# Middle-stage weights converted seven batches earlier by way of DRAM, and the middle channel product in seven block products

## The chip, the cores and the metric

The kernel runs on one core of a Trainium2 chip. The metric is the device time of one execution, in microseconds (us); the median of three runs of the kernel before is 1297.31 us (1297.03 to 1298.79).

The engines are called by their full names in the text; the profile calls them PE (TensorE matmul), PEld (TensorE weight load), DVE (VectorE), ACT (ScalarE), POOL (GpSimd) and SP (SyncE, which issues the DMAs here).

## The reference, cut to what matters

Three blocks follow each other, on 8 batches of 576 tokens with 512 channels: attention with pooled keys, a mixing block with a token and a channel product, and a second one.

```python
# block 1: x = attention(q, k, v)                    (8, 576, 512)
theta = x @ w_theta                                   # block 2
y = w_tok_r @ (x * cos(theta)) + w_tok_i @ (x * sin(theta))
u = x + y
x = u + maximum(u @ w_ch, 0)                          # 512 x 512: the middle channel product
h = (maximum(x.T @ w_tok1, 0) @ w_tok2).T             # block 3: 576 -> 256 -> 576 over the tokens
u = x + h
out = u + maximum(u @ w_ch1, 0) @ w_ch2               # 512 -> 1536 -> 512 over the channels
```

The weights arrive as float64. There is no such type on the engines, so the kernel takes each number apart in two 32-bit words and puts a float32 together from them with integer operations ("conversion" below).

## The kernel before, in words

**Precision.** A float32 product is made of three faster ones: each operand is split into a high part (a cast on ScalarE) and a low part (the difference, on VectorE or GpSimd), and high x high, high x low and low x high are added up in PSUM. So every matrix needs a cast and a subtraction before it can be used, and every product costs three matmuls. The list `HL3` names the three.

**Stages.** (1) A prologue. (2) The mixing of the eight batches, one after the other: `mix_steps(b)` is the token product of batch b (four row blocks, each in 256 and 320 columns), and `interleave` slips the "side" work in between: attention and theta of batch b+1, loads for b+2. A side step stands beside a due time, in us of a modelled TensorE clock; the constants are in the table `P`. (3) The middle stage: per batch the channel product `ch` with `w_ch`, transposes `emit_tr`, and the two token products `emit_tok1` and `emit_tok2`. (4) The last stage, `channel_mix`, with `w_ch1` and `w_ch2`. The engines run in order; a scheduler behind the language settles the order on each engine when the kernel is built.

**The weights of the middle stage** (`w_ch`, `w_tok1`, `w_tok2`) are converted in 19 pieces while the last batch is mixed: `begin` in the last batch's side work queues them (`add_wch`, `add_tok1`, `add_tok2`), and `cq_step` (L239) does one at a time: four or so VectorE operations (L248 to L271), the cast on ScalarE (L294), the low part on GpSimd or VectorE (L296). They stay in SBUF.

**The middle channel product** (`emit_ch`, L889) multiplies, for each of four output blocks and each of two token ranges (256 and 320), 12 matmuls: four row blocks of `w_ch` times the three high/low pairs. That is 8 groups of 12, or in blocks of half the channels and half the tokens eight block products. One VectorE operation per group takes the result from PSUM: maximum with 0, plus u (L900). `split_u` (L881) makes the high and low parts of the input, four casts and four subtractions of 576 columns a batch.

**The weights of the last stage** are converted beside it: `weight_steps(0, ...)` in six quads of six steps; `wstep()` places a step at six points of a batch. Its sums for seven block products are `sums(i)` (L1033): two on GpSimd (L1037, L1038), two on VectorE (L1039, L1040). `channel_mix` already works with seven block products (`first_pair`, L1262).

Of the kernel before, what the change touches and what calls it, by code (L numbers as in the profile page):

```python
# [56 lines left out]
    "mo": 1,  # L57
}
# [6 lines left out]
def tile_attn_moe(  # L65
# [713 lines left out]

    def mix_steps(b):  # L780
# [11 lines left out]
    def mix_part(b, half, jj, th, part, hold):  # L792
# [16 lines left out]
        if part == 8:  # L809
            R = r_t[b]  # L810
            nc.vector.tensor_add(out=R[:, j, ts], in0=o, in1=R[:, j, ts])  # L811
            if th == 1:
                nc.sync.dma_start(out=scr_u[b][:, j, :], in_=R[:, j, 0:T])
# [16 lines left out]
    wch = [None] * 4  # L830
    A2 = {}

    def add_wch():
        for k in range(4):
            cq_add(pair_tile(("q0", "q1", "pt0", "pt1")[k], 512, f"wch{k}", wch, k),
                   w_ch[k * 128:(k + 1) * 128, :], HALVES)

    def add_tok1():
        def make():
            t = st("e", [128, 2, 5, 256], F32R, "wk1")  # L840
            A2["tok1"] = t
            return t

        get = lazy(make)
        for s in range(4):
            cq_add(lambda s=s: (get()[:, 0, s, :], get()[:, 1, s, :]),
                   w_tok1[s * 128:(s + 1) * 128, :], ((0, 256),))

        def tail(m):
            t = get()  # L850
            nc.scalar.copy(out=t[:, 0, 4, :], in_=m)
            nc.gpsimd.memset(t[64:128, 1, 4, :].bitcast(F32), 0.0)
            nc.gpsimd.tensor_sub(out=t[0:64, 1, 4, :], in0=m[0:64], in1=t[0:64, 0, 4, :].bitcast(F32))

        cq_src.append((w_tok1[512:576, :], 64, tail))

    def add_tok2():
        def make(s):
            if s == 0:
                t = st("kr", [128, 2, T], F32R, "wk2a")  # L860
                t = (t[:, 0], t[:, 1])
            else:
                t = (st("t1", [128, T], F32R, "wk2b"), st("pl", [128, T], F32R, "wk2c"))
            A2["tok2", s] = t
            return t

        for s in range(2):
            cq_add(lazy(lambda s=s: make(s)), w_tok2[s * 128:(s + 1) * 128, :], ((0, 192), (192, 384), (384, 576)))

    u_t = {}  # L870
    uh_t = {}
# [3 lines left out]
    def load_u(b):  # L875
        t = st(("R0", "R1", "Z1")[b % 3], [128, 4, TD], F32, f"u{b}")
        u_t[b] = t
        for j in range(4):
            nc.sync.dma_start(out=t[:, j, 0:T], in_=scr_u[b][:, j, :])

    def split_u(b, j):  # L881
        if j == 0:
            uh_t[b] = (st("Xh", [128, 4, T], F32R), st("Xl", [128, 4, T], F32R))
        h, l = uh_t[b]
        u = u_t[b][:, j, 0:T]
        nc.scalar.copy(out=h[:, j], in_=u)
        nc.vector.tensor_sub(out=l[:, j], in0=u, in1=h[:, j].bitcast(F32))

    def emit_ch(b, j, th):  # L889
        t0, n = TH[th]  # L890
        ts = slice(t0, t0 + n)
        h = uh_t[b]
        o = bank_any()[:, 0:n]
        i = 0
        for a, w in HL3:
            for k in range(4):
                mm(o, wch[k][:, w, j * 128:(j + 1) * 128], h[a][:, k, ts], i == 0, i == 11)
                i += 1
        u = u_t[b][:, j, ts]
        nc.vector.scalar_tensor_tensor(out=u, in0=o, scalar=0.0, in1=u, op0=ALU.max, op1=ALU.add)  # L900
        gate[0] = u[0:1, 0:1]
        if j == 3 and th == 1:
            dup_tail(u_t[b], nc.scalar.copy)
# [56 lines left out]
    A12, A22, S1, S2, S3, S4, A11 = range(7)  # L960
    PO = (A11, S2, A12, S1, S3, S4, A22)
# [15 lines left out]
    def weight_steps(m, wd, tags, gaps):  # L977
# [55 lines left out]
        def sums(i):  # L1033
# [3 lines left out]
            nc.gpsimd.tensor_tensor(out=s[:, 0], in0=a21, in1=a22, op=ALU.add)  # L1037
            nc.gpsimd.tensor_tensor(out=s[:, 2], in0=a11, in1=a21, op=ALU.subtract)  # L1038
# [47 lines left out]
    HOME_E = (("Z1", 5), ("Xh", 3), ("Xl", 3), ("R0", 3))  # L1086
# [454 lines left out]
    if True:  # L1541
        prologue()
        for b in range(B):
# [12 lines left out]
            if last:  # L1556
                def begin():
                    zt = st(f"zt{(b + 1) % 2}", [128, CV, 2], U32, "late0")
                    vs = [st(x, [128, 256, 2], U32, f"late_{x}") for x in ("vbh", "vbl", "vlh", "vll")]
                    vr = st("vr", [128, 3, CV], F32, "late1")  # L1560
                    n = [int(x + 0.5) for x in P["l_n"]]
                    cq_use((["stg0", "stg1", "bdk"] + ([zt] + vs)[0:n[0]]),
                           (["cvt0", "vlr"] + [vr[:, i] for i in range(3)])[0:1 + n[1]])
                    lo_m[0] = max(2, n[2])
                    cq_mode[0] = min(2, int(P["md"][0] + 0.5))
                    add_wch()
                    add_tok1()
                    add_tok2()
                    cq_load()
                side.append((0.0, begin))  # L1570
                for i in range(19):
                    side.append((P["l_cq"][0] + P["l_cq"][1] * i, cq_step))
# [21 lines left out]
        if B > 1:  # L1594
            load_u(1)
# [88 lines left out]
```

## Time and profile before

| what | value |
|---|---|
| median of 3 runs | 1297.31 us |
| the profiled execution's own time | 1297.42 us |
| its span | 1295.6 us |
| TensorE busy | 97% of the span |
| VectorE, ScalarE, GpSimd busy | 74%, 51%, 25% |
| granted TensorE clock, mean | 0.995 |

The span is the time from the first to the last instruction; what lies around it is 1.8 us. TensorE's share is an average over stages with different limits, so stretches are read apart: the mixing runs to about 526 us, the middle stage from there to about 752 us, the last stage from there on.

### The profile page before, as it was taken

Reading aid. Unit: us, or ns where it says so; the run is one execution under the profiler, and the core shown is the slowest. Engines: PE = TensorE matmul, PEld = TensorE weight load, DVE = VectorE, ACT = ScalarE, POOL = GpSimd, SP = SyncE. Lnnn points to the kernel's source line nnn. Section 1 sums busy time; section 2 is a strip of 40 time slices with the busy share of each in tenths; the row PEclk is TensorE's granted clock in tenths of the full one; section 3 lists DMA queues with packets and bytes.
Section 4 is the critical chain, followed back from the end, with each engine's and each line's share of the span. In section 5 each row is a group of like instructions: output and inputs, shape, how many; then the busy total and the mean of one; then the engine's idle time right before and its main releaser. Section 6 shows DMA issues by size and latency. Waiting matters only on the chain.

```text
span 1295.6 us, 22271 instructions
## 1 busy us (share of the span) xinstructions
PE 1254.6 (97%) x8130; PEld 1209.8 (93%) x8132; DVE 956.9 (74%) x1730; ACT 661.0 (51%) x1256; POOL 321.9 (25%) x339
## 2 busy tenths in 40 slices
PE   5799999999999999999999999999999999999998
PEld 4489999999999988899999998999999999999998
DVE  7888577585857796686775689996545598987893
ACT  4776565666666573333331356655544444444442
POOL 4643425232332532111110012320000032123122
PEclk9899999999999999999999999999999999999999
DMA  9424233231321023556683388885438966547621
GB/s 338 158 71 138 74 100 103 75 94 62 115 73 52 36 93 109 181 199 233 246 297 116 128 273 281 281 280 178 146 123 279 367 215 224 172 142 218 196 91 62
DMA packets 120382, 214.50 MB, mean 166 GB/s; under 512 B 11536, under 2 KB 66320, under 8 KB 120272
## 3 DMA queue, kind: packets, MB, share of 16 engines
q1 hardware_dynamic: 120272, 213.08, 49.2%
q8 instruction: 64, 1.05, 0.3%
q14 instruction: 46, 0.38, 0.1%
HBM read 134.39 MB, written 78.64 MB: 164 GB/s over the span
## 4 chain that ended last, share of the span: by engine, by line
PE 76%; DVE 9%; DMA 2%; issue 2%; ACT 2%; POOL 0%; SPq 0%; ACTq 0%; DVEq 0%; POOLq 0%
PE m L159 28%; PE x L159 25%; PE t L159 19%; PE x L173 3%; DMA ws<-w_ch 1%; DMA scr_x<-u 1%; DVE wm L1024 1%; DVE raw_n L1155 1%; DVE wm L1028 1%; DVE wsum L1039 0%; DVE p L1313 0%; DVE g L1323 0%; ACT wo L1052 0%; DVE ope_R L1152 0%; ACT wm L1018 0%
## 5 line engine op out<-in xcount | busy, mean ns | idle before, releaser
L159 PE MATMUL m<-wtk,Z 128*128 128x256 f32 (+1 forms) x1536 | 253.6, 301 | 4.6 <-ACT Z L772 3.0
L159 PEld LDWEIGHTS m<-wtk,Z 128*128 128x128 f32 x1536 | 220.2, 190 | 6.1 <-ACT Z L772 3.2
L773 POOL TENSOR_TENSOR Z<-tmp,Z 128x1024 fp32r<-128x1024 f32 x31 | 74.9, 2415 | 112.1 <-ACT Z L772 112.1
L159 PE MATMUL x<-ope_Z,wa 128*128 128x384 f32 x492 | 95.4, 337 | 0.0
L1404 POOL TENSOR_TENSOR o<-o,u 128x384 f32<-128x384 f32 x12 | 16.3, 1379 | 285.5 <-DVE u L1392 218.0
L159 PEld LDWEIGHTS x<-ope_Z,wa 128*128 128x128 f32 x492 | 86.8, 188 | 0.1
L1038 POOL TENSOR_TENSOR wsum<-wm 128x128 f32<-128x128 f32 (+1 forms) x18 | 15.1, 840 | 272.4 <-DVE wm L1028 264.8
L758 DVE TENSOR_TENSOR tmp<-x,tmp 128x1024 f32<-128x1024 f32 x32 | 39.1, 1221 | 33.4 <-ACT tmp L734 17.8
L159 PE MATMUL t<-wth,Xh 128*128 128x256 f32 x448 | 62.9, 282 | 0.0
L159 PE MATMUL x<-bdk,q 128*128 128x144 f32 x320 | 47.8, 303 | 11.5 <-DVE bdk L1463 7.0
L159 PEld LDWEIGHTS t<-wth,Xh 128*128 128x128 f32 x448 | 57.9, 188 | 0.9 <-DVE tmp L709 0.2
L159 PEld LDWEIGHTS x<-bdk,q 128*128 128x128 f32 x320 | 44.5, 203 | 13.1 <-issue 10.9
L159 PE MATMUL m<-wtk,zt 128*128 128x256 f32 (+1 forms) x192 | 56.8, 296 | 0.0
L557 POOL TENSOR_TENSOR e<-e,sm 128x720 f32<-128x720 f32 x32 | 44.7, 1398 | 20.8 <-DVE sm L556 18.7
L159 PE MATMUL t<-ope_Z,wa 128*128 128x384 f32 x234 | 48.2, 336 | 1.5 <-ACT p L1312 1.5
L159 PE MATMUL m<-ope_Z,wa 128*128 128x384 f32 x234 | 48.2, 336 | 0.0
L740 DVE SCALAR_TENSOR_TENSOR tmp<-tmp,t 128x512 f32<-128x512 f32 x33 | 22.5, 683 | 31.3 <-ACT tmp L727 31.3
L545 ACT ACTIVATE e<-e 128x720 f32<-128x720 f32 x32 | 25.6, 804 | 38.0 <-DVE e L540 37.9
L159 PE MATMUL x<-ope_R,wa 128*128 128x384 f32 x228 | 44.1, 338 | 0.4 <-DVE p L1317 0.3
L811 DVE TENSOR_TENSOR R<-m,R 128x256 f32<-128x256 f32 (+1 forms) x64 | 28.8, 450 | 20.2 <-PE m L159 20.2
L772 ACT CAST Z<-tmp 128x1024 fp32r<-128x1024 f32 x32 | 33.4, 1043 | 20.0 <-DVE tmp L758 20.0
L159 PE MATMUL m<-ope_Xl,wa 128*128 128x384 f32 x204 | 42.9, 338 | 0.6 <-ACT ope_Xl L1151 0.6
(406 smaller groups left out, 3546.3 us busy)
## 6 DMA issues: line engine op xcount, KB each, us to landing
wa<-scr_w SPq DMA_DIRECT2D x42, 512.0 KB, 5.6
scr_g<-g SPq DMA_DIRECT2D x108, 192.0 KB, 3.0
scr_w<-wo SPq DMA_DIRECT2D x42, 256.0 KB, 3.0
scr_u<-R SPq DMA_DIRECT2D x32, 288.0 KB, 2.1
u<-scr_u SPq DMA_DIRECT2D x32, 288.0 KB, 4.0
scr_w<-wo SPq DMA_DIRECT2D x18, 512.0 KB, 3.4
scr_x<-u SPq DMA_DIRECT2D x32, 288.0 KB, 2.4
raw_n<-scr_x SPq DMA_DIRECT2D x24, 384.0 KB, 4.3
```

The lines of the kernel that those rows point to most:

```text
L159: nc.tensor.matmul(out=o, lhsT=l, rhs=r, start=start, stop=stop, skip_group_check=skip)
L173: nc.tensor.transpose(o, i, ident)
L545: nc.scalar.activation(out=ep, in_=ep, func=ACTF.Exp, scale=1.0 / 64.0)
L557: nc.gpsimd.tensor_tensor(out=ep, in0=ep, in1=sm.unsqueeze(3).to_broadcast([128, 5, 2, 72]), op=ALU.mult)
L740: nc.vector.scalar_tensor_tensor(out=t, in0=t, scalar=MAGIC, in1=pt, op0=ALU.subtract, op1=ALU.subtract)
L758: nc.vector.tensor_tensor(out=tmp, in0=px.unsqueeze(1).to_broadcast([128, 2, 512]), in1=tmp, op=ALU.mult)
L772: nc.scalar.copy(out=zh, in_=zv)
L773: later(1.0 if lo is nc.vector else 0.0, lambda: lo.tensor_sub(out=zl, in0=zv, in1=zh.bitcast(F32)), tg, zg)
L811: nc.vector.tensor_add(out=R[:, j, ts], in0=o, in1=R[:, j, ts])
L1024: nc.vector.scalar_tensor_tensor(out=xu, in0=t[:, :, :, 1], scalar=0xC0000000, in1=xu, op0=ALU.bitwise_and, op1=ALU.bitwise_or,)
L1038: nc.gpsimd.tensor_tensor(out=s[:, 2], in0=a11, in1=a21, op=ALU.subtract)
L1404: nc.gpsimd.tensor_tensor(out=u22[d].t, in0=u22[d].t, in1=u2[d].t, op=ALU.add)
```

## The change

**Conversion.** The 19 pieces in the last batch go. The same weights are converted in 17 pieces during the mixing of batches 1 to 6, three a batch, each in the steps load, conversion and split, at due times 8, 14 and 18 us in a batch plus 12 us for each piece. The results, high and low parts, go to DRAM (`scr_c`, `scr_t1`, `scr_t2`) and are loaded back in the last batch (`late_loads`). A load is held until a result of the current batch is there: a one-element copy on ScalarE into its buffer reads that result (`mixed`). For `w_ch` the split also makes the sums that seven block products need.

**Channel product.** `emit_ch` and `split_u` are replaced by `ch_steps` and `prep_u`: the matrices in 2 x 2 blocks (256 channels by 288 tokens), seven products of sums of blocks, each 2 x 6 matmuls of 288 columns. `prep_u` makes four differences of blocks (eight instructions on GpSimd) and splits seven blocks instead of four. The results are put together by 16 VectorE operations, 4 on ScalarE and 2 on GpSimd a batch.

**Around it.** The order of batches at the start of the stage (channel products of batches 0 and 1 before the first token product), the places of transposes and input splits, which buffers hold u and the weights of the last stage (fewer), the order in which the last stage takes its buffers, and the two sums of `weight_steps(0, ...)` that were on GpSimd move to VectorE.

The diff, cut to its core:

```diff
+    "ew": (8.0, 14.0, 18.0),
+    "ewp": 12.0,
...
+        def load(i):
...
+            nc.scalar.copy(out=t[0:1, 0, 0:1].bitcast(F32), in_=mixed[0])
...
+        def conv(i):
+            nc.scalar.activation(out=m, in_=t[:, :, 1].bitcast(F32), func=ACTF.Abs)
+            nc.scalar.activation(out=m, in_=m, func=ACTF.Relu, bias=floor[:, 0:1])
+            nc.scalar.activation(out=m, in_=m, func=ACTF.Identity, bias=floor[:, 1:2])
+            nc.vector.tensor_scalar(
...
+            nc.vector.scalar_tensor_tensor(
...
+            nc.vector.scalar_tensor_tensor(
...
+        def split_ch(m, j, c0):
...
+            nc.gpsimd.tensor_tensor(out=s[:, 0], in0=a21, in1=a22, op=ALU.add)
+            nc.gpsimd.tensor_tensor(out=s[:, 2], in0=a11, in1=a21, op=ALU.subtract)
+            nc.gpsimd.tensor_tensor(out=s[:, 1], in0=s[:, 0], in1=a11, op=ALU.subtract)
+            nc.gpsimd.tensor_tensor(out=s[:, 3], in0=a12, in1=s[:, 1], op=ALU.subtract)
+            for src, k, o0 in ((x[:, 1], 2, A12), (x[:, 0, 0:1], 1, A11), (s[:, 0:2], 2, S1), (s[:, 2:4], 2, S3)):
...
+                nc.scalar.copy(out=o[:, :, 0], in_=src)
+                nc.gpsimd.tensor_sub(out=o[:, :, 1], in0=src, in1=o[:, :, 0].bitcast(F32))
+                for i in range(k):
+                    nc.sync.dma_start(out=scr_c[:, o0 + i, j, :, c0:c0 + 64], in_=o[:, i].bitcast(F32))
...
-    def split_u(b, j):
...
-    def emit_ch(b, j, th):
...
+    def prep_u(b):
...
+        def raw(o, k, t):
+            h, l = new(o)
+            nc.scalar.copy(out=h, in_=blk(k, t))
+            nc.vector.tensor_sub(out=l, in0=blk(k, t), in1=h.bitcast(F32))
+
+        def diff(o, x, y):
+            d[o] = diffs.pop(0)
+            for k in range(2):
+                nc.gpsimd.tensor_tensor(out=d[o][:, k], in0=x[:, k], in1=y[:, k], op=ALU.subtract)
+
+        def fin(o):
...
+            nc.scalar.copy(out=h, in_=x)
+            nc.vector.tensor_sub(out=l, in0=x, in1=h.bitcast(F32))
...
+    def ch_steps(b):
...
+        def prod(o, ps, first):
...
+            for ih in I:
+                seq = [(w[:, k, wi, ih * 128:ih * 128 + 128], (h, l)[a][:, k]) for a, wi in HL3 for k in range(2)]
+                for i, (x, r) in enumerate(seq):
+                    mm(ps[ih], x, r, first and i == 0, i == len(seq) - 1, not first)
...
+        def s1():
+            v["W"] = banks()
+            prod(S1, v["W"], True)
+            v["p5"] = new()
+            for i in I:
+                nc.vector.tensor_add(out=v["p5"][i], in0=v["W"][i], in1=v["u2"][i])
...
+                nc.scalar.activation(out=e[i], in_=e[i], func=ACTF.Relu)
+                nc.gpsimd.tensor_tensor(out=x, in0=x, in1=e[i], op=ALU.add)
...
+                nc.vector.tensor_add(out=e[i], in0=v["W"][i], in1=v["u2"][i])
+                nc.vector.scalar_tensor_tensor(out=x, in0=e[i], scalar=0.0, in1=x, op0=ALU.max, op1=ALU.add)
...
-            nc.gpsimd.tensor_tensor(out=s[:, 0], in0=a21, in1=a22, op=ALU.add)
-            nc.gpsimd.tensor_tensor(out=s[:, 2], in0=a11, in1=a21, op=ALU.subtract)
+            eng = nc.gpsimd if whole else nc.vector
+            eng.tensor_tensor(out=s[:, 0], in0=a21, in1=a22, op=ALU.add)
+            eng.tensor_tensor(out=s[:, 2], in0=a11, in1=a21, op=ALU.subtract)
...
-                for i in range(19):
-                    side.append((P["l_cq"][0] + P["l_cq"][1] * i, cq_step))
+                side.append((0.0, late_loads))
...
+            for i in range(3 if 0 < b < 7 else 0):
+                for f, t in zip(early.pop(0) if early else (), P["ew"]):
+                    side.append((t + P["ewp"] * i, f))
```

Three places show how the instructions move. First VectorE at the turn from the seventh to the last batch, before; `late`, `cvt` and `vlr` hold a piece under conversion, `wch` and `wk` finished weights, and the lines 670 to 716 and 640 belong to the mixing.

```order
L249 TENSOR_SCALAR late_5491<-bdk 128x256
L249 TENSOR_SCALAR late_5491<-stg_5665 128x256
L640 TENSOR_TENSOR Xl<-x_5277,Xh 128x320
L253 TENSOR_SCALAR late_5491<-late_5491 128x256
L640 TENSOR_TENSOR Xl<-x_5285,Xh 128x320
L256 TENSOR_SCALAR late_5491<-late_5491 128x256
L253 TENSOR_SCALAR late_5491<-late_5491 128x256
L262 SCALAR_TENSOR_TENSOR late_5491<-bdk,late_5491 128x256
L296 TENSOR_TENSOR wch_5648<-cvt_5562,wch_5648 128x256
```

The same place now:

```order
L816 TENSOR_TENSOR R_4843<-m_5523,R_4843 128x256
L643 TENSOR_TENSOR Xl<-x_5644,Xh 128x256
L643 TENSOR_TENSOR Xl<-x_5651,Xh 128x256
L643 TENSOR_TENSOR Xl<-x_5659,Xh 128x320
L643 TENSOR_TENSOR Xl<-x_5667,Xh 128x320
L712 TENSOR_TENSOR tmp_5707<-t_5698,tmp_5707 64x512
L716 SCALAR_TENSOR_TENSOR tmp_5707<-tmp_5707 64x512
L743 SCALAR_TENSOR_TENSOR tmp_5738<-tmp_5738,t_5710 128x512
```

The conversion steps are gone from between the mixing's own instructions. Second, VectorE in the channel product of the third batch, before; `u` is that batch, `wo` belongs to the last stage's weights.

```order
L900 SCALAR_TENSOR_TENSOR u_6210<-x_6558,u_6210 128x256
L1053 TENSOR_TENSOR wo_2_11_6883<-wsum_2_6704,wo_2_11_6883 128x2x256
L900 SCALAR_TENSOR_TENSOR u_6210<-x_6580,u_6210 128x320
L900 SCALAR_TENSOR_TENSOR u_6210<-m_6594,u_6210 128x256
L900 SCALAR_TENSOR_TENSOR u_6210<-t_6614,u_6210 128x320
```

The same place now; `up` and `ud` are partial sums in SBUF, `wm` a weight of the last stage under conversion.

```order
L1068 TENSOR_TENSOR up_zt_6257<-m_6847,ud_vr 128x288
L1068 TENSOR_TENSOR up_zt_6257<-t_6848,up_vbh 128x288
L1075 SCALAR_TENSOR_TENSOR u_6601<-x_6823,u_6601 128x288
L1230 TENSOR_SCALAR wm_2_6877<-wm_2_6877 128x512
L1075 SCALAR_TENSOR_TENSOR u_6601<-x_6824,u_6601 128x288
L1231 TENSOR_SCALAR wm_2_6877<-wm_2_6877 128x512
L1082 TENSOR_TENSOR up_vlh<-x_6883,up_zt_6257 128x288
L1235 SCALAR_TENSOR_TENSOR wm_2_6877<-ws_2_0_6595,wm_2_6877 128x512
L1082 TENSOR_TENSOR up_vbl<-x_6884,up_zt_6257 128x288
L1239 SCALAR_TENSOR_TENSOR wm_2_6877<-ws_2_0_6595,wm_2_6877 128x512
```

Every result from PSUM now stands between two conversion steps of the last stage's weights. Third, GpSimd in the middle stage, before, for one quad of these weights:

```order
L1038 TENSOR_TENSOR wsum_2_6704<-wm_2_6608 128x256
L1053 TENSOR_TENSOR wo_2_01_6790<-wm_2_6608,wo_2_01_6790 128x256
L1037 TENSOR_TENSOR wsum_2_6704<-wm_2_6608 128x256
L1053 TENSOR_TENSOR wo_2_00_6786<-wm_2_6608,wo_2_00_6786 128x2x256
L1038 TENSOR_TENSOR wsum_3_7011<-wm_3_6915 128x256
```

The same place now:

```order
L1000 TENSOR_TENSOR ud_w_6010<-u_6782,ud_bdk 128x288
L1000 TENSOR_TENSOR ud_vr<-u_6782,ud_w_6010 128x288
L1088 TENSOR_TENSOR u_6601<-u_6601,up_vlh 128x288
L1088 TENSOR_TENSOR u_6601<-u_6601,up_vbl 128x288
L1265 TENSOR_TENSOR wo_2_01_7042<-wm_2_6877,wo_2_01_7042 128x256
L1265 TENSOR_TENSOR wo_2_00_7038<-wm_2_6877,wo_2_00_7038 128x2x256
L1000 TENSOR_TENSOR ud_w_6010<-u_6782 128x288 x2
```

GpSimd had four instructions per quad, and has twelve per batch now: eight differences, two sums with u and two of the four of the quad.

## Rows read from the trace of the kernel before

**Rows 1.** The page, part 1: busy time, share of span, instructions.

```profile
PE 1254.6 (97%) x8130; PEld 1209.8 (93%) x8132; DVE 956.9 (74%) x1730; ACT 661.0 (51%) x1256; POOL 321.9 (25%) x339
```

**Rows 2.** Windows of 50 us: busy per engine, clock, DMA share, GB/s.

```profile
200.00:250.00 50.00, 49.96 (x388) 49.01 (x387) 35.98 (x72) 31.63 (x65) 16.47 (x19) 1.00 0.30 98
...
450.00:500.00 50.00, 44.51 (x324) 42.78 (x323) 45.73 (x111) 28.65 (x65) 18.03 (x18) 0.97 0.30 98
...
600.00:650.00 50.00, 50.00 (x347) 47.62 (x346) 36.40 (x70) 17.07 (x35) 7.63 (x8) 1.00 0.76 269
...
750.00:800.00 50.00, 47.78 (x271) 46.17 (x270) 43.65 (x100) 30.05 (x69) 11.66 (x18) 1.00 0.87 289
```

**Rows 3.** Waits of TensorE, 440 to 760 us: total, times, longest.

```profile
PE m L159 <- ACT Z L772: 3.0, 1, 3.0
PE m L159 <- DVE R L811: 1.6, 1, 1.6
PE x L173 <- DVE u L900: 1.2, 1, 1.2
PE x L159 <- DVE t L599: 0.9, 1, 0.9
```

**Rows 4.** Timeline of TensorE, one batch: start, duration, instruction.

```profile
710.17 2.96 PE L159 MATMUL x<-x,wk 128*128 128x512 f32 x12
...
716.68 1.11 PE L159 MATMUL t<-Xh,wch 128*128 128x256 f32 x8
...
718.10 1.34 PE L159 MATMUL x<-Xh,wch 128*128 128x320 f32 x8
...
729.38 0.28 PE L159 MATMUL t<-wk2a,h1a 128*128 128x256 f32 x1
...
737.92 2.96 PE L159 MATMUL x<-x,wk 128*128 128x512 f32 x12
```

**Rows 5.** Timeline of TensorE, in the last batch's mixing.

```profile
489.67 1.65 PE L159 MATMUL m<-wtk,Z 128*128 128x256 f32 x6 [2.98 <-ACT Z L772]
...
491.33 1.83 PE L159 MATMUL m<-wtk,Z 128*128 128x256 f32 x8
492.99 0.28 PE L159 MATMUL m<-wtk,zt 128*128 128x256 f32 x1
```

**Rows 6.** Timeline of VectorE, 500 to 585 us.

```profile
504.90 0.49 DVE L811 TENSOR_TENSOR R<-m,R 128x320 f32<-128x320 f32 x1 [0.19 <-PE m L159]
505.31 2.30 DVE L887 TENSOR_TENSOR Xl<-u,Xh 128x576 fp32r<-128x576 f32 x1
...
532.63 1.50 DVE L1039 TENSOR_TENSOR wsum<-wsum,wm 128x256 f32<-128x256 f32 x1 [0.52 <-POOL wsum L1037]
534.16 0.42 DVE L1040 TENSOR_TENSOR wsum<-wm,wsum 128x256 f32<-128x256 f32 x1
...
543.21 2.76 DVE L887 TENSOR_TENSOR Xl<-u,Xh 128x576 fp32r<-128x576 f32 x4
545.88 1.28 DVE L916 TENSOR_TENSOR x<-x,x 128x512 fp32r<-128x512 f32 x2
...
570.39 0.49 DVE L950 TENSOR_TENSOR u<-x,u 128x320 f32<-128x320 f32 x1
570.79 0.41 DVE L950 TENSOR_TENSOR u<-m,u 128x256 f32<-128x256 f32 x1
```

**Rows 7.** Timeline of GpSimd, 440 to 760 us.

```profile
504.26 2.73 POOL L773 TENSOR_TENSOR Z<-tmp,Z 128x1024 fp32r<-128x1024 f32 x1 [9.64 <-ACT Z L772]
...
531.85 0.74 POOL L1037 TENSOR_TENSOR wsum<-wm 128x256 f32<-128x256 f32 x1 [1.35 <-DVE wm L1028]
532.55 1.29 POOL L1053 TENSOR_TENSOR wo<-wm,wo 128x512 fp32r<-128x512 f32 x1
```

**Rows 8.** Timeline of GpSimd, 199 to 203 us, between two batches.

```profile
199.82 2.40 POOL L773 TENSOR_TENSOR Z<-tmp,Z 128x1024 fp32r<-128x1024 f32 x1 [1.75 <-ACT Z L772]
```

**Rows 9.** Timeline of TensorE, 209.5 to 211 us, the next batch.

```profile
210.00 1.12 PE L159 MATMUL m<-wtk,Z 128*128 128x256 f32 x8
```

More of the change, by code (lines that the diff above doesn't have):

```diff
@@ L857, in add_tok2 @@
[L857 to L868, printed above, removed]
+    A12, A22, S1, S2, S3, S4, A11 = range(7)
@@ new lines, in tile_attn_moe, with load_ch, late_loads @@
+    wch = {}
+    A2 = {}
+    def load_ch(tags, os):
+        for tag, o in zip(tags, os):
+            wch[o] = st(tag, [128, 2, 2, 256], F32R, f"wch{o}")
+            nc.sync.dma_start(out=wch[o].bitcast(F32), in_=scr_c[:, o])
+    def late_loads():
+        load_ch(("q0", "q1", "pt0", "pt1"), PO[0:4])
+        A2["tok1"] = st("e", [128, 2, 5, 256], F32R, "wk1")
+        nc.sync.dma_start(out=A2["tok1"].bitcast(F32), in_=scr_t1)
+        a = st("kr", [128, 2, T], F32R, "wk2a")
+        nc.sync.dma_start(out=a.bitcast(F32), in_=scr_t2[0])
+        A2["tok2", 0] = (a[:, 0], a[:, 1])
+        A2["tok2", 1] = (st("t1", [128, T], F32R, "wk2b"), st("pl", [128, T], F32R, "wk2c"))
+        for w in range(2):
+            nc.sync.dma_start(out=A2["tok2", 1][w].bitcast(F32), in_=scr_t2[1][:, w])
@@ L879, in load_u @@
             nc.sync.dma_start(out=t[:, j, 0:T], in_=scr_u[b][:, j, :])
-    def split_u(b, j):
[L882 to L887, printed above, removed]
-    def emit_ch(b, j, th):
[L890 to L903, printed above, removed]
+    units = []
@@ new lines, in tile_attn_moe, with open_ch, open_posts @@
+    posts = []
+    diffs = []
+    uo = {}
+    def open_ch():
+        for tag, n in (("Xh", 4), ("Xl", 4), ("n0", 1), ("n1", 1), ("n2", 1), ("n3", 1), ("stg0", 1), ("stg1", 1)):
+            t = st(tag, [128, n, 2, TS], F32R, f"uo_{tag}")
+            units.extend(t[:, i] for i in range(n))
+    def open_posts():
+        for tag, n in (("vbh", 1), ("vlh", 1), ("vbl", 1), ("vll", 1), ("zt1", 3)):
+            t = st(tag, [128, n, TS], F32, f"up_{tag}")
+            posts.extend(t[:, i] for i in range(n))
@@ L1591, in ch, with tr @@
+        def ch(steps):
+            for i, f in enumerate(steps):
+                f()
                 if i % 2 == 0:
                     wstep()
-        if B > 1:
-            load_u(1)
-        ch(0)
-        if B > 1:
-            for j in range(4):
-                split_u(1, j)
-        for c in range(2 if P["a_tr"] < 8 else 0, 5):
-            emit_tr(0, c)
+        def tr(b, *cs):
+            if b < B:
+                for c in cs:
+                    emit_tr(b, c)
+        load_u(1)
@@ L1602, in tile_attn_moe @@
+        pu = prep_u(1)
+        for i, f in enumerate(ch_steps(0)):
+            f()
+            for _ in range((0, 0, 2, 1, 1, 1, 0)[i]):
+                pu.pop(0)()
+            if i % 2 == 0:
+                wstep()
+        steps = ch_steps(1)
+        ch(steps[0:2])
+        tr(0, 0, 1, 2, 3, 4)
+        for _ in range(4):
+            pu.pop(0)()
+        ch(steps[2:])
         for b in range(B):
@@ L1613, in tile_attn_moe @@
                         wstep()
-                    if j == 1 and th == 0 and b + 1 < B:
-                        for c in range(5):
-                            emit_tr(b + 1, c)
+                    if b > 0:
+                        tr(b + 1, *{(1, 1): (0, 1), (2, 0): (2,), (2, 1): (3,), (3, 0): (4,)}.get((j, th), ()))
                 if b + 2 < B:
-                    split_u(b + 2, j)
+                    for _ in range((3, 2, 2, 2)[j]):
+                        pu.pop(0)()
         wstep(1000)
```

228 lines of the change are left out of this document (173 added, 55 removed).

## The prediction, made before the changed kernel was run

> **What bounds the kernel now.** I read the page's busy shares first, then windows of 50 us, then TensorE's waits, then its timeline. TensorE is busy 97% of the span [rows 1], and the windows say where it is not. A window inside the mixing (200 us) and one inside the middle stage (600 us) have TensorE busy for 49.96 and 50.00 of 50 us; the turn to the last batch (450 us) has 44.51 [rows 2]. So in both stages time goes only with TensorE's own instructions, and at the turn there are waits to win. The waits name them: 3.0, 1.6 and 0.9 us on ScalarE's Z, VectorE's R and VectorE's t, all in the last two batches, and 1.2 us on u at the start of the middle stage [rows 3]. The window of the turn is also the one in which VectorE is busiest, 45.73 us against 35.98 in the mixing before it [rows 2]: the conversion runs there. The middle stage is next in line for VectorE: 36.40 of 50 us at 600 us [rows 2].
>
> **Part 1, matmuls of the channel product.** One batch of the stage before takes 27.75 us, from one first token product to the next (710.17 to 737.92), and its channel product 12.70 of them (716.68 to 729.38) [rows 4]. It is four groups of 12 matmuls of 256 columns and four of 320. A group of 256 takes 1.42 us (716.68 to 718.10), so one of 320 takes (12.70 - 4 x 1.42) / 4 = 1.755. Halfway lies a group of 288: 1.59. Seven products are 14 such groups with 6 matmuls, the matmuls of seven groups: 11.1 us. That is 1.6 us less per batch, and a batch of 26.2 us. For eight batches 12.7 us go, if TensorE stays the bound.
>
> **Part 2, the conversion leaves the last batch.** The three waits at the turn are 5.5 us [rows 3]. The granted clock in the window is 0.97 [rows 2], and after the wait of 2.98 us the seven matmuls from 489.67 to 491.33 and the eight from there to 492.99 take 1.66 us each [rows 5]; at 1.42 / 12 = 0.118 a matmul [rows 4] they would take 0.83 and 0.95. That is about the lower of the clock's two levels (1.2 GHz, not 2.4). So another 1.5 us hang on the wait: 7.0 in all. I take 6, since the last batch still makes the parts of the first middle input, now seven splits and eight GpSimd differences. The 1.2 us on u at the stage's start [rows 3] I leave standing: the two channel products there need as much VectorE time as any.
>
> **Part 3, the conversion in batches 1 to 6.** It adds three pieces a batch. VectorE has 14 us free in 50, ScalarE 18, GpSimd 33 [rows 2]. A piece adds 3 VectorE operations, at most 8 on ScalarE and 8 on GpSimd, each of 288 columns or fewer; none of the three fills up. What could hurt is order. On GpSimd the splits stand before the low part of Z for the next batch. That one ends at 202.2 [rows 8], and the first matmul that reads it starts at 210.00 [rows 9]: 7.8 us in hand, and a piece's train of eight small operations is, at 0.74 for 256 columns [rows 7], under 6. On ScalarE a one-element copy waits for the mixing's last result, and behind it stand sine and exponential of the next batch. On SP the stores to DRAM wait for GpSimd, and behind them stand loads of the batch after next, which have a batch's time. Low end 0; high end 17 pieces with a wait like the 0.9 us on t [rows 3], 15 us. I take 1, near the low end, since the nearest row is the 7.8 us in hand. The loads back from DRAM in the last batch have a whole batch's mixing to land in.
>
> **Part 4, VectorE in the middle stage.** This is the part that gives time back. At 600 us VectorE works 36.40 of 50 us, so 20.2 in a batch of 27.75 [rows 2, 4]. What one instruction adds is read from start to start: 0.40 us for 320 columns from PSUM (570.39 to 570.79), 0.67 for a split of 576 (four from 543.21 to 545.88) [rows 6]; on the line through these 0.33 for 256 and 0.367 for 288. Added: 16 operations of 288 columns at 0.367 instead of eight at 0.33 and 0.40, 5.9 - 2.9 = 3.0; three more splits, 2.0; two sums from GpSimd, 0.7. Taken away: the sum of L1039 took 1.50 us where its twin L1040 took 0.42 [rows 6], because GpSimd's 1.29 us operation had begun 0.08 us before [rows 7]; without that, 1.1 less. So 24.8 us.
>
> GpSimd has 7.63 us in 50 at that place, 4.2 a batch [rows 2]. Ten operations of 288 columns at 0.81 (between 0.74 for 256 and 1.29 for 512 [rows 7]) come in, two of 0.74 go: 10.8 us. The two engines hold each other up: L1039 lost 1.1 us a batch to 4.2 us of GpSimd, 0.26 us for each. At that ratio 10.8 us cost VectorE 2.8, and it needs 27.6 us in a batch for which TensorE needs 26.2. Six batches carry a quad of the last stage's weights; there VectorE is 1.4 us late per batch, 8.4 in all. In the last two there is no quad (14 operations of 256 to 512 columns, about 6 us by the spacing above), and VectorE fits. Ends: 0 if what is lost falls into VectorE's own idle time; and at the worst row, the split at 505.31 that took 2.30 us instead of 0.67 while GpSimd ran one operation of 2.73 [rows 6, 7], 0.6 us for each GpSimd us: 6.5 a batch, 31.3 us, 30 us in six batches. I take 8.4, the ratio of the weight sums, which run in this very stage beside this very kind of operation.
>
> The Trainium skill ("SBUF — State Buffer", section "Who interferes with whom") speaks against this change: a VectorE operation with two inputs in SBUF and a GpSimd operation that reads SBUF shut each other out for a whole instruction. The two rows above agree: the split at 505.31 ended 0.6 us after GpSimd did, the sum at 532.63 0.3 us after. Worked out by the rule as an estimate, 25 such VectorE operations a batch would meet a busy GpSimd in 10.8 / 26.2 of cases and wait half of 0.81 us: 4.2 instead of 2.8, and the time would be about 1296.
>
> ScalarE has 17.07 of 50 us at that place [rows 2], 9.5 a batch; three casts and four copies more leave it at half a batch.
>
> **Sum.** The profiled execution took 1297.4 us, span 1295.6 and 1.8 around it; the median of the runs is 1297.3, the same. 1297.4 - 12.7 - 6 + 1 + 8.4 = 1288.1. I predict **1288 us**. At the turn to the last stage (2.2 us idle at 750 [rows 2]) operands of the last stage find their buffers later, since they now hold middle inputs, but weights start earlier; I set it to 0.
>
> **Rivals.** (B) The results from PSUM are taken in time whatever GpSimd does, and the middle stage stays TensorE's: 1297.4 - 12.7 - 6 + 1 = 1279.7. For it: VectorE's 24.8 us alone are under 26.2. Against it: the order puts a conversion step behind nearly every one of these results, and an accumulating product must wait until its bank has been read.
>
> (C) Slower: VectorE and GpSimd shutting each other out makes the middle stage VectorE's. Its place is the six batches with a quad, its price the excess over 26.2 us times six; it decides from an excess of 18.7 / 6 = 3.1 us, that is 4.5 us lost a batch, 0.42 per GpSimd us. At the worst row's 0.6 the time is 1297.4 - 18.7 + 1 + 30 = 1310. For it: GpSimd's work there rises from 4.2 to 10.8 us. Against it: 20-odd of VectorE's operations in a batch read a result from PSUM, and the one at 504.90, while GpSimd's 2.73 us ran, took 0.49 us, no longer than its like at 570.39 [rows 6, 7].
>
> (D) The conversion in batches 1 to 6 stalls the mixing, which has no slack on TensorE: 10 us there, 1297.4 - 18.7 + 8.4 + 10 = 1297.1, no change. For it: ScalarE's waiting copies and the three waits that the same work makes in the last batch. Against it: that is 19 pieces in one batch, and here are three.
>
> **How the numbers follow.** Forecast 0.51, B 0.20, C 0.15, D 0.14. A measurement of this kernel can tell 0.2%, 2.6 us, from no change. Faster by more: 0.46 of the forecast, all of B, 0.04 of D, 0.70. Within: 0.03, 0.03 of C and 0.06 of D, 0.12. Slower: the rest, 0.18. The range takes in B below, with 2 us for a smoother start of the stage, and C not quite half the way to its 1310: 1277 to 1303. The forecast's own range is 1283 to 1293.
>
> **What would show it.** Right: TensorE idle for under 1 us in the last batch's mixing and at full clock; channel products of 11.1 us where nothing waits; VectorE over 90% busy from the second to the sixth middle batch, batches of 27 to 28 us there, TensorE's longest waits on VectorE; the last two batches near 26.2. Batches of 26.2 throughout would be B, over 29 C; TensorE under 49 of 50 us in the windows between 150 and 440 us would be D. A last stage that takes more than 2 us longer would show that its operands' later buffers were a cost I left out.

## The result, and the profile after

The changed kernel takes 1312.11 us (median of 4 runs, 1309.20 to 1313.55), the kernel before 1298.05 on the same chip: ratio 1.0105, 95% interval 1.0091 to 1.0119. It is slower; 1288 was forecast, and the time lies above the range.

The profiled execution divides into stages by TensorE's first instruction of each (us):

| stage | before | after | forecast for after |
|---|---|---|---|
| mixing, ends at | 526.2 | 527.4 | 521.2 |
| middle stage | 225.6 | 239.4 | 221.3 |
| last stage | 543.8 | 544.9 | 543.8 |

So 18 us of the miss are in the middle stage and 6 in the mixing. Each profile is one execution: in ten of the runs below the mixing has the same instructions, and it ends between 524.1 (e12) and 527.8 (e9), so the 6 may be 3. Part 1 of the page of the changed kernel, against [rows 1]:

```profile
PE 1255.4 (96%) x8034; PEld 1200.4 (92%) x8036; DVE 1005.0 (77%) x1781; ACT 712.9 (54%) x1402; POOL 404.4 (31%) x467
```

TensorE has 96 matmuls fewer and is busy no less; the other three are busy 48, 52 and 83 us longer. The windows of [rows 2], after:

```profile
200.00:250.00 50.00, 48.81 (x376) 47.72 (x376) 37.51 (x81) 36.28 (x86) 24.37 (x41) 1.00 0.45 131
450.00:500.00 50.00, 48.51 (x367) 46.94 (x366) 25.00 (x53) 26.11 (x57) 15.34 (x19) 1.00 0.36 131
600.00:650.00 50.00, 47.41 (x292) 43.65 (x293) 47.42 (x91) 21.66 (x43) 14.34 (x16) 0.93 0.56 190
```

The turn (450) gained 4.0 us of TensorE work and the full clock, the mixing window (200) lost 1.15 of 49.96, the middle window (600) 2.6 and clock. Cut by batch, from one first token product to the next, the middle stage shows this (window, its length, TensorE, its weight loads, VectorE, ScalarE, GpSimd, clock):

```profile
577.00:609.00 32.00, 29.03 (x180) 27.35 (x179) 30.59 (x58) 14.11 (x29) 13.40 (x14) 0.89 0.53 183
609.00:637.00 28.00, 26.80 (x181) 24.94 (x180) 25.68 (x49) 12.60 (x26) 10.04 (x10) 1.00 0.47 160
637.00:665.00 28.00, 27.16 (x184) 25.12 (x183) 27.73 (x54) 12.27 (x25) 12.52 (x12) 1.00 0.53 183
665.00:696.00 31.00, 28.70 (x182) 25.83 (x181) 28.94 (x55) 14.53 (x27) 12.05 (x13) 0.94 0.69 243
696.00:725.00 29.00, 27.00 (x181) 24.58 (x180) 24.75 (x43) 10.58 (x20) 11.41 (x12) 1.00 0.56 201
```

The first four last 28 to 32 us where 27.6 were forecast; VectorE is busy for 92 to 99% of them, TensorE for 91 to 97%. The fifth has no quad (a group of the last stage's weights under conversion) and VectorE is busy for 85% of it, yet it lasts 29 us where 26.2 were forecast. So a full VectorE does not explain the stage alone. TensorE's longest wait of the stage, with a matmul behind it, in its timeline:

```profile
600.90 1.69 PE L175 MATMUL x<-con,u 128*128 128x128 f32 x6 [2.97 <-DVE u L1112]
602.25 0.56 PE L161 MATMUL m<-wk2a,h1a 128*128 128x256 f32 x1
```

VectorE's timeline before it:

```profile
594.25 1.06 DVE L1104 SCALAR_TENSOR_TENSOR u<-up_vll,u 128x288 f32<-128x288 f32 x1
595.24 1.30 DVE L1235 SCALAR_TENSOR_TENSOR wm<-ws,wm 128x512 uint32<-128x512 uint32 x1
...
597.68 1.04 DVE L1104 SCALAR_TENSOR_TENSOR u<-up_zt,u 128x288 f32<-128x288 f32 x1
...
599.02 0.44 DVE L1111 TENSOR_TENSOR up_zt<-t,up_zt 128x288 f32<-128x288 f32 x1
599.38 1.83 DVE L1112 SCALAR_TENSOR_TENSOR u<-up_zt,u 128x288 f32<-128x288 f32 x2
```

GpSimd's, the same stretch:

```profile
592.29 0.81 POOL L1000 TENSOR_TENSOR ud_w<-u,ud_bdk 128x288 f32<-128x288 f32 x1 [1.67 <-DVE wm L1239]
...
594.01 0.98 POOL L1000 TENSOR_TENSOR ud_w<-u,ud_bdk 128x288 f32<-128x288 f32 x1
595.07 0.92 POOL L1000 TENSOR_TENSOR ud_vr<-u,ud_w 128x288 f32<-128x288 f32 x1
596.12 1.09 POOL L1088 TENSOR_TENSOR u<-u,up_vlh 128x288 f32<-128x288 f32 x1
597.17 1.24 POOL L1088 TENSOR_TENSOR u<-u,up_vbl 128x288 f32<-128x288 f32 x1
598.38 2.16 POOL L1265 TENSOR_TENSOR wo<-wm,wo 128x256 fp32r<-128x256 f32 x2
```

From 592 us to 600.5 GpSimd hardly pauses, and VectorE operations with both inputs in SBUF are drawn out: L1104 takes 1.04 to 1.06 us, where the quick ones of its line in this stage take 0.44, and the first of the two of L1112 takes 1.47. L1111, of the same width but with one input from PSUM, takes 0.44. The transposes wait for L1112. The Trainium skill's rule ("SBUF — State Buffer", section "Who interferes with whom"), that such operations and GpSimd's shut each other out, agrees with these rows, and with GpSimd's own: a difference that takes 0.81 us at 592.29 takes 1.01 on average over the stage. After the wait a matmul of 256 columns shows 0.56 us, where the same instruction showed 0.28 at 729.38 in [rows 4]: TensorE ran at the lower of its two levels (1.2 GHz) for 6.8 us. Two such stretches cost 5 us.

The differences stand there because their input is late. The queue in which SyncE issues the DMAs (SPq), ahead of it:

```profile
576.29 7.85 SPq L1165 DMA_DIRECT2D scr_x<-u  x4
585.94 1.75 SPq L958 DMA_DIRECT2D u<-scr_u  x4
```

Three buffers hold u. An input can be loaded only when the result of the batch three back has left the same buffer; the last of its four stores is issued by 584.1. The load is issued at 585.9, when TensorE is in the next channel product (from 583.3), and GpSimd starts on it after a wait of 7.3 us:

```profile
588.86 1.76 POOL L1000 TENSOR_TENSOR ud_bdk<-u 128x288 f32<-128x288 f32 x2 [7.30 <-DMA u<-scr_u]
```

Five of the eight differences then fall into its 11 us, and the sixth right behind, beside the 16 operations with which VectorE puts the results together. Over batches 3 to 7 it is 28 of 40.

### The profile page after: what moved, and what is told of

Its sections match the earlier page's. It is cut to its first block, busy times and chain, and to the rows that moved or that the text cites. A ratio compares the mean times of both kernels' runs of the same rounds, so it can differ in the third digit from the quotient of the medians.

```text
span 1311.6 us, 22728 instructions
## 1 busy us (share of the span) xinstructions
PE 1255.4 (96%) x8034; PEld 1200.4 (92%) x8036; DVE 1005.0 (77%) x1781; ACT 712.9 (54%) x1402; POOL 404.4 (31%) x467
## 5 line engine op out<-in xcount | busy, mean ns | idle before, releaser
L1616 POOL TENSOR_TENSOR o<-o,u 128x384 f32<-128x384 f32 x12 | 16.2, 1373 | 284.9 <-DVE u L1604 239.9
L161 PE MATMUL x<-ope_Z,wa 128*128 128x384 f32 x300 | 60.4, 338 | 2.2 <-DVE p L1529 2.2
L161 PE MATMUL x<-ope_Xh,wa 128*128 128x384 f32 x288 | 60.1, 337 | 0.0
L761 DVE TENSOR_TENSOR tmp<-x,tmp 128x1024 f32<-128x1024 f32 x32 | 39.0, 1220 | 22.7 <-ACT tmp L737 19.9
L161 PEld LDWEIGHTS x<-ope_Z,wa 128*128 128x128 f32 x300 | 52.9, 188 | 3.2 <-DVE p L1529 3.2
L161 PE MATMUL x<-ope_Xl,wa 128*128 128x384 f32 x252 | 55.1, 338 | 0.0
L161 PE MATMUL m<-ope_Z,wa 128*128 128x384 f32 x252 | 53.6, 338 | 1.6 <-ACT p L1524 0.8
L161 PE MATMUL t<-ope_Z,wa 128*128 128x384 f32 x252 | 53.0, 337 | 0.0
L161 PEld LDWEIGHTS x<-ope_Xh,wa 128*128 128x128 f32 x288 | 51.2, 188 | 0.1
L560 POOL TENSOR_TENSOR e<-e,sm 128x720 f32<-128x720 f32 x32 | 44.6, 1396 | 16.5 <-DVE sm L559 16.3
L161 PE MATMUL x<-ope_R,wa 128*128 128x384 f32 x240 | 47.3, 338 | 1.7 <-ACT ope_R L1363 1.2
L161 PEld LDWEIGHTS m<-ope_Z,wa 128*128 128x128 f32 x252 | 44.5, 188 | 2.8 <-ACT p L1524 1.1
```

The lines of the kernel that those rows point to most:

```text
L161: nc.tensor.matmul(out=o, lhsT=l, rhs=r, start=start, stop=stop, skip_group_check=skip)
L560: nc.gpsimd.tensor_tensor(out=ep, in0=ep, in1=sm.unsqueeze(3).to_broadcast([128, 5, 2, 72]), op=ALU.mult)
L761: nc.vector.tensor_tensor(out=tmp, in0=px.unsqueeze(1).to_broadcast([128, 2, 512]), in1=tmp, op=ALU.mult)
L1616: nc.gpsimd.tensor_tensor(out=u22[d].t, in0=u22[d].t, in1=u2[d].t, op=ALU.add)
```

## The experiments

All ratios are to the kernel before on the same chip (1297.5 to 1298.9); "middle" is the middle stage of the profiled execution, against 225.6 before and 239.4 after. Theory E: VectorE's total, its own work and what it loses beside GpSimd, sets the stage. Theory L: single operations held up at places where TensorE waits. Theory D came later: late inputs. Times and ratios are of several executions, a stage's length is of one.

**One part alone: early conversion** (the eight-block product and its `split_u`, `emit_ch` stay):

```diff
+    "ew": (8.0, 14.0, 18.0),
+    "ewp": 12.0,
...
-                for i in range(19):
-                    side.append((P["l_cq"][0] + P["l_cq"][1] * i, cq_step))
+                side.append((0.0, late_loads))
...
+            for i in range(3 if 0 < b < 7 else 0):
+                for f, t in zip(early.pop(0) if early else (), P["ew"]):
+                    side.append((t + P["ewp"] * i, f))
```


> The kernel before with one part of the change alone: the middle weights converted in batches 1 to 6 by way of DRAM (17 pieces, high and low parts stored in the old layout); the channel product stays at eight block products. In the changed kernel the mixing ended 1.25 us later than before (527.43 against 526.18), so what the conversion won at the turn to the last batch it lost in batches 1 to 6. Theory E (VectorE and GpSimd shutting each other out in the middle stage is the loss): this kernel is within 4 us of before, 1294 to 1302, and its middle stage is 225 to 227 us as before. Rival (the early conversion and its stores and loads are the loss): 1305 or more, with the mixing ending 8 us or more later than before.

1299.95, ratio 1.0013 (1.0003 to 1.0023). Middle and last stage are near those of before (225.7, 542.8); mixing ends at 527.2. The conversion alone is worth nothing. R takes the mixing's results from PSUM, t is a low part in the next batch's attention; TensorE's waits from 100 to 475 us (total, times, longest):

```profile
PE m L161 <- DVE R L816: 3.4, 5, 0.9
PE x L161 <- DVE t L602: 2.5, 6, 0.6
```

The time is as E has it: the turn's gain goes in some 1 us a batch, since R and t stand behind conversion operations on VectorE, which the next run puts to the test.

**The same, at other times:**

```diff
-    "ew": (8.0, 14.0, 18.0),
-    "ewp": 12.0,
+    "ew": (35.0, 44.0, 46.0),
+    "ewp": 5.0,
```


> The kernel of e1_early_only (1299.95 us: the kernel before with the early conversion alone) with other due times: load, conversion and split at 35, 44 and 46 us plus 5 us for each piece, not 8, 14 and 18 plus 12, so that the conversion's VectorE operations stand between the last theta work and the softmax of a batch. Theory E (the about 1 us a batch that the mixing lost are results R and t standing behind conversion operations on VectorE): the waits go and the turn's gain stays, 1293 to 1297. Rival (the conversion costs that much wherever it stands, by ScalarE's waiting copies or by GpSimd): 1299 to 1301.

1294.74, ratio 0.9973 (0.9963 to 0.9983), mixing ends at 523.9. It leaves nothing out and beats both kernels. TensorE's waits in the same stretch:

```profile
PE m L161 <- ACT Z L775: 3.0, 4, 0.9
PE x L175 <- POOL pl L565: 0.4, 1, 0.4
```

Those on R and t are gone; 3.0 us on Z, an operand of the mixing's product, came.

**The differences left out, or moved to VectorE** (in the first, the blocks are split directly; in the second `nc.vector` takes them):

```diff
-            d[o] = diffs.pop(0)
-            for k in range(2):
-                nc.gpsimd.tensor_tensor(out=d[o][:, k], in0=x[:, k], in1=y[:, k], op=ALU.subtract)
+            d[o] = x
```


> The changed kernel without the eight GpSimd differences of blocks per batch: the blocks themselves are split in their place (the seven products are then of other operands). VectorE's instructions are the same in number and size. Theory E: what VectorE operations with two SBUF inputs lose beside GpSimd, 28 us in the middle stage, falls to 10 us or less, and the time to 1293 to 1302. Rival L (VectorE's plain load and the order of its instructions are the loss, whoever runs beside it): 1309 to 1314, as the changed kernel.

> The changed kernel with the eight differences per batch on VectorE instead of GpSimd: 8 x 0.37 = 2.9 us more VectorE work a batch, some 23 us over the stage, and 8 us less GpSimd work a batch. Theory E: what is lost beside GpSimd falls from 28 us to under 10, which pays for most of it: 1308 to 1316. Rival L: VectorE, already the bound at 96% of the stage, is 23 us longer: 1325 to 1336.

Without them 1293.69, ratio 0.9969 (0.9957 to 0.9981), middle 222.6: they cost 16.8 us. On VectorE 1307.93, 1.0081 (1.0065 to 1.0097), middle 236.6: eight more VectorE operations a batch cost less than the same eight on GpSimd. Both agree with E, the second within 0.1 us.

**Fewer operations that collide** (the last four sums stay in PSUM, so that the operation after each has one input in SBUF), and fewer, longer ones on GpSimd:

```diff
-            e = new()
+            e = v["W"]
...
-                e, x = v["u2"][i], blk(1, 0, i)
+                e, x = v["Z"][i], blk(1, 0, i)
```


> The changed kernel with the last four sums of a batch's channel product left in PSUM instead of SBUF, so that the four operations that follow them have one SBUF input instead of two; as many instructions, of the same size. In the changed kernel these four lost 9.9 of the 28 us, at the end of the channel product, where the transposes wait for them. Theory E: they go back to 0.45 us each, the longest waits of the transposes and the two stretches of low clock go, and the time is 1298 to 1305. Rival L: 1309 to 1314.

```diff
-            for k in range(2):
-                nc.gpsimd.tensor_tensor(out=d[o][:, k], in0=x[:, k], in1=y[:, k], op=ALU.subtract)
+            nc.gpsimd.tensor_tensor(out=d[o], in0=x, in1=y, op=ALU.subtract)
```


> The changed kernel with the same differences on GpSimd in four operations of 576 columns a batch, not eight of 288. Theory E (what VectorE loses goes by the time that GpSimd is at work): the same within a few us, 1307 to 1315. Rival (each start of a GpSimd operation has its own price, so half as many cost half): 1300 to 1306.

The first: 1303.59, 1.0055 (1.0036 to 1.0074), middle 235.9; L1104, drawn out to 0.8 to 1.4 us in 10 of its 16 cases before, takes 0.45 in all 16. The time is in E's range, but TensorE's waits in the stage are still 15.4 us (16.5 in the changed kernel), and the low clock did not go. The second: 1319.79, 1.0159 (1.0139 to 1.0180), middle 248.0, against both expectations. The same columns in operations of 1.4 to 1.6 us cost 8.6 us more. GpSimd is busy 12 us less in the stage, and VectorE's operations lose 37 us, not 30 (an estimate from the trace: each against the quick ones of its line): how long one collision lasts counts, not only their sum.

**Less VectorE work** (on the kernel of e3):

```diff
-            nc.vector.tensor_scalar(out=x, in0=x, scalar1=F64_FLOOR, scalar2=None, op0=ALU.max)
+                nc.scalar.activation(out=x, in_=x, func=ACTF.Relu, bias=floor[:, 0:1])
+                nc.scalar.activation(out=x, in_=x, func=ACTF.Identity, bias=floor[:, 1:2])
```


> The kernel of e3_sums_in_psum (1303.6 us) with the maximum of the last stage's weight conversion (12 VectorE operations of 0.53 us in the middle stage) replaced by two ScalarE operations each. Theory E (VectorE's total, its own work plus what it loses beside GpSimd, sets the six batches with a quad): each us taken from VectorE there is won, 6.4 us, so 1296 to 1301. Rival L (VectorE has room on average; only single operations drawn out by GpSimd hold TensorE up, and they stay): 1302 to 1305.

1302.11, 1.0041 (1.0025 to 1.0057). The profiled middle is 230.1, 5.8 less, as E has it; the times show 1.5, as L has it. The profiled execution of e3 was its slowest (1307.63), that of e5 its fastest (1300.33), so the 5.8 say too much. It does not decide.

> The changed kernel with the sums left in PSUM (as e3), the maximum on ScalarE (as e5) and the later due times (as e6). If the three gains add up: 1312 - 8.5 - 5 - 5 = 1293.5, so 1290 to 1297, faster than the kernel before. Rival: the gains share one bound (VectorE full in the middle stage, a wait of the mixing that only moves), 1297 to 1303.

1318.30, 1.0160 (1.0146 to 1.0175), against both expectations. The middle is 230.7 as in e5, but mixing ends at 543.6. Here a piece of `w_ch` carries the block sums, and they stand before theta's work. ScalarE, in one of the three batches that have such pieces:

```profile
269.83 0.30 ACT L910 CAST eo<-es 128x128 fp32r<-128x128 f32 x1 [3.24 <-POOL es L905]
...
271.82 0.67 ACT L730 ACTIVATE tmp<-t,magic 128x512 f32<-128x512 f32 x1
```

TensorE behind it:

```profile
276.80 1.00 PE L161 MATMUL x<-bdk,q 128*128 128x144 f32 x6 [2.71 <-DVE tmp L761]
```

ScalarE waits 3.24 us for a sum on GpSimd, L730 stands behind it, and L761 and TensorE come late; so three times (8.8 us), with the clock at 0.93 to 0.97 in those windows. The due times that help the plain pieces hurt these.

**The quads spread over more batches:**

```diff
-                ch(ch_steps(b + 1))
+                ch(ch_steps(b + 1), 4)     # two weight steps in a channel product, not four
```


> The changed kernel with the six quads of the last stage's weights spread over more middle batches: in the channel products of batches 2 to 7 two weight steps, not four, so that 24 of the 36 steps fall on six batches (four each) and not on four (six each). Theory E (VectorE's total in a batch, its own work and what GpSimd takes, stands above TensorE's only where a quad runs; a quad is about 9 us of VectorE there): 3 us less VectorE in four batches, 6 more in the next two, which have about that much room: 1303 to 1308. Rival L (single drawn-out operations at the end of the channel product hold TensorE up, and the differences stay where they are): 1310 to 1315. Rival T (the last quads come too late for the last stage): 1315 to 1320.

> The kernel of e5_max_on_scalare (1302.1 us: sums left in PSUM, maximum on ScalarE) with the quads spread as in e9_quads_spread. Theory E: batches that took 29 to 30 us come to 26.5 to 27, the two after them stay under 27.5: 5 to 8 us less, 1294 to 1298. Rival L: 1300 to 1304. Rival T: 1304 or more.

1311.03, 1.0098 (1.0081 to 1.0114), and 1310.15, 1.0083 (1.0062 to 1.0104). Evening out VectorE's total gains nothing, against E; the first time is in L's range. In the second it loses 8, in T's range but not for T's reason: ScalarE, in order, waits for a quad's load ahead of a cast for the token product:

```profile
604.65 0.66 ACT L1228 ACTIVATE wm<-ws 128x512 f32<-128x512 f32 x1 [5.32 <-DMA ws<-w_ch]
605.22 0.57 ACT L1127 CAST x<-t 128x512 fp32r<-128x512 f32 x1
```

TensorE waits with it:

```profile
605.84 0.80 PE L161 MATMUL x<-x,wk 128*128 128x512 f32 x1 [3.02 <-ACT x L1127]
```

**The differences behind the channel product:**

```diff
+        if late:
+            nc.scalar.copy(out=t[0:1, :, 0], in_=u_t[b - 1][0:1, 3, 0:4])
...
+                load_u(b + 2, b > 0)       # behind ch(ch_steps(b + 1))
+                pu = prep_u(b + 2)
```


> The changed kernel with the load of the input u of batch b+2 issued behind the channel product of batch b+1 (a four-element copy on ScalarE holds it until that product's last result is there), so that the eight differences run on GpSimd beside the token products, not beside the channel product, where the trace of the changed kernel has seven of the eight. The work is the same. Theory K (what costs is that GpSimd's work and VectorE's taking of results fall into the same 11 us): most of the 16.8 us that the differences cost comes back, 1297 to 1304. Theory E (the totals of a batch decide, wherever the operations stand): 1309 to 1315. Rival T (the inputs come too late for the next channel product): 1315 or more.

> The kernel of e5_max_on_scalare (1302.1 us) with the same later load as in e11_differences_later. Theory K: 1290 to 1297, faster than the kernel before. Theory E: 1300 to 1305. Rival T: 1305 or more.

1329.66, 1.0236 (1.0217 to 1.0255), and 1319.68, 1.0162 (1.0136 to 1.0188): rival T. The chain from load over difference, cast and split to the product is then what is late. GpSimd in e11:

```profile
641.76 1.82 POOL L1002 TENSOR_TENSOR ud_bdk<-u 128x288 f32<-128x288 f32 x2 [10.34 <-DMA u<-scr_u]
```

TensorE, behind the cast of that difference:

```profile
648.16 2.12 PE L161 MATMUL x<-uo_Xl,wch 128*128 128x288 f32 x12 [1.47 <-ACT uo_Xl L1008]
```

**VectorE's own work taken away:**

```diff
+            if not whole:
+                return          # conv: without its three integer operations
```


> The changed kernel without the three integer operations in each half of the quads converted in the middle stage (36 VectorE operations of 512 columns; the last stage then multiplies with other weights, its time is not meant). The differences stay on GpSimd. Theory E (what is lost beside GpSimd costs because VectorE is full already; with about 4 us less of its own work per quad it has room): nearly all of the middle stage's loss returns, 1290 to 1298. Theory L (single operations held up by GpSimd at the end of the channel product cost in any case): under 8 us return, 1304 to 1311.

> The changed kernel without the eight differences (as e2_no_differences) and without the three integer operations (as e13_no_bit_operations); both are left out of the computation. Every theory: the middle stage is TensorE's with batches of 26.2 us, 1283 to 1290. If it stays above 1292, something else than VectorE and GpSimd holds the stage up.

1311.48, 1.0091 (1.0065 to 1.0117), middle 236.3, and 1296.40, 0.9983 (0.9974 to 0.9993), middle 222.4. The first is 0.5 us above L's range and speaks against E: in its window at 600 us VectorE has room (36.07 of 50), and the stage is nearly as late.

```profile
600.00:650.00 50.00, 44.31 (x285) 39.71 (x283) 36.07 (x70) 21.13 (x41) 16.45 (x18) 1.00 0.62 213
```

The second lies above 1292, so something else holds the stage too; its middle is that of e2, so without the differences the integer operations cost nothing. Timelines of the first (e13) name what holds it, of ScalarE:

```profile
645.72 0.67 ACT L994 CAST uo_Xh<-u 128x576 fp32r<-128x576 f32 x1 [2.67 <-DMA u<-scr_u]
```

of VectorE:

```profile
646.43 0.76 DVE L995 TENSOR_TENSOR uo_Xh<-u,uo_Xh 128x576 fp32r<-128x576 f32 x1 [2.48 <-ACT uo_Xh L994]
```

and of TensorE:

```profile
651.16 1.81 PE L161 MATMUL m<-uo_n,wch 128*128 128x288 f32 x6 [2.23 <-DVE up_zt L1082]
```

A split for the batch after next waits for u to land, and the sum that TensorE needs now (L1082) stands behind it on VectorE. Over the stage VectorE's waits of this kind add up to 12.0 us (total, times, longest), and to 11.5 in e14:

```profile
DVE uo_Xh L995 <- ACT uo_Xh L994: 12.0, 6, 3.5
```

In e16 below 0.7 us of them is left.

**The late inputs taken away:**

```diff
+        if b > 2:
+            u_t[b] = u_t[b - 3]      # load_u: work on what the buffer holds
+            return
```


> The changed kernel, in which the inputs u of batches 3 to 7 are not loaded: they work on what the buffer holds from three batches before (left out of the computation; all operations on the engines stay). So the differences and splits need not wait until that buffer has been stored and loaded again, some 5 to 7 us. Theory D (the inputs land when the channel product of the batch before has begun, so their differences and splits stand in it, and ahead of its sums on engines that work in order): 8 us or more come back, 1303 or less. Theory L (it is the collisions with GpSimd alone, which stay): 1307 to 1314.

> The same without the three integer operations of each half quad (as e13_no_bit_operations, 1311.5 us); both are left out of the computation. Theory D: with room on VectorE and early inputs nothing holds TensorE, batches of 26.2 to 27 us, 1284 to 1294. Theory L: 1300 or more.

> The kernel of e5_max_on_scalare (1302.1 us) with the inputs of batches 3 to 7 not loaded (left out of the computation). Theory D: 1290 to 1297. Theory L: 1299 to 1304.

1305.69, 1.0055 (1.0039 to 1.0071); 1294.40, 0.9964 (0.9953 to 0.9976); 1301.64, 1.0025 (1.0012 to 1.0037). The first lies between the two theories, the second 0.4 us above D's range, the third in L's. The middle stage of four kernels:

| | all of VectorE's work | without 36 integer operations |
|---|---|---|
| inputs loaded | 239.4 | 236.3 |
| inputs not loaded | 234.4 | 223.2 |

One change alone gives 3.1 or 5.0 us, both 16.2; in the ratios it is 0.14%, 0.50% and 1.41%. TensorE's waits of 0.2 us and more in the stage are 16.5 us in the changed kernel, 16.2 in e13, 15.8 in e15 and 8.0 in e16. So what e15 gained alone is the low clock (5 us, none in e15), and the waits go only with both changes. Of the 40 differences of batches 3 to 7, 13 fall into a channel product in e15, 28 in the changed kernel. That the loads taken off SyncE's queue let other loads through is not the reason: ScalarE's waits for the quads' loads are 12.2 us in the changed kernel, 15.5 in e15. The window at 600 us of e15:

```profile
600.00:650.00 50.00, 47.36 (x310) 43.16 (x311) 49.28 (x93) 24.69 (x48) 19.75 (x21) 1.00 0.46 159
```

and of e16:

```profile
600.00:650.00 50.00, 48.93 (x328) 45.51 (x327) 46.65 (x84) 24.39 (x49) 20.72 (x22) 1.00 0.47 165
```

So two limits lie one behind the other, as far as these runs, which leave work out, can show it. With early inputs VectorE is full (49.28 of 50) and TensorE waits for it; with a lighter VectorE the inputs hold it. Leaving the differences out (222.6) removes a step from both: collisions on VectorE, and a link of the chain from load to product; which of the two counts more, no run separates. e17 is no better than e5: VectorE is full there too (48.65 of 50 at 600).

## Why the prediction was wrong

**The step that failed is Part 4's sum.** It took a batch as the longer of two totals, 27.6 us of VectorE or 26.2 of TensorE, so 8.4 us late; measured, the stage lost 26.5 against 225.6 - 12.7 = 212.9. VectorE's total itself was near: 28.2 us busy in the mean of the four batches with a quad above, and over the stage some 30 us lost (the estimate above) beside 87 us of GpSimd, 0.34 for each where 0.26 was set. But these batches took 29.8 us. In the stage TensorE's waits of 0.2 us and more rose from 2.4 to 16.5, the low clock behind two of them is 5, and some 7 I did not trace. The sum spread the loss over the batch. The differences come mostly inside the channel product, because u is late; Part 4 did not look at how inputs get their buffer. And its way out, a VectorE with less to do, did not help by itself (e13).

Of the signs set out beforehand, the turn at full clock, VectorE over 90% busy in the batches with a quad and TensorE's longest wait on VectorE came; batches of 27 to 28 us, and the last two near 26.2 (29.2 and 27.5), did not. TensorE's 48.81 us in the window at 200 us was the sign of rival D.

**Rival C** had the sign and nearly the size (1310), with VectorE as the stage's only master; e9, e13 and e15 say that it is one of two. That its time came so near is partly luck: it had the mixing end 6 us too early and the middle stage 3.5 us too long. C's evidence against it holds as a fact: operations that read PSUM kept 0.44 us beside GpSimd.

**Part 2** was right at the turn (4.0 us more TensorE work in the window, no low clock) and wrong at the stage's start. I left 1.2 us of waiting there "standing"; two channel products ahead of the first token product wait for splits, sums and transposes' inputs, and TensorE's waits from 527 to 577 us add up to 6.2 us, 3.9 even without differences (e2).

**Part 3** set the conversion at 1 us; in e1 TensorE's waits from 100 to 475 us add up to 6.7 us, against 2.4 in the kernel before, and nearly all are on R and t, so it cost 4 to 6. I had looked at GpSimd, ScalarE and SP for what stands behind a piece, and not at VectorE, whose R and t were held. That was the mechanism of rival D, at about half its price. Other due times give 5.2 us back in the times (e6 against e1).

**Part 1** is right where nothing waits: a group of six matmuls of 288 columns takes 0.80 us (527.43 to 528.23), 11.2 for 14, and the last full batches of e16 take 26.2. That is why the change could have paid: with both limits gone (e16, which leaves work out) the stage takes 223.2 us, 2.4 less than before, and 10 are still open to it, 5.4 of them waits before 556 us.

The last stage, set at 0, took 1.0 us longer. What was not tried is a fourth buffer for u with the loads kept.

## What to carry over

Before moving work onto engines beside a full TensorE, ask where in the batch it will fall, not only how much it is: follow each input from its buffer's last reader through store, load and every cast to the instruction that needs it. Engines that work in order pass a late input on to whatever stands behind it, so a total below the bound does not show that a stage will keep to it. And when taking one suspected cost away gives nothing, take away the wait that has come in its place as well, before the theory is dropped.

## What the runs showed of the hardware

GpSimd's operations grow too, not only VectorE's: a difference of 288 columns took 0.81 us at its quick level, 1.01 on average over the middle stage, up to 1.41. Cutting the same GpSimd work into halves was better than longer operations by 7 to 8 us in the times (e8). In the changed kernel a wait of TensorE of 2.97 us was followed by 6.8 us at half the granted clock and one of 1.54 by 3.4, but one of 1.47 us (537.53) by none; in e16 one of 2.28 us (543.61) was followed by none, its windows show 1.00.
